# Output sums in the seats of layer A's rows, and one model of the shared port in a planned two-layer attention kernel

## The chip, the core and the metric

The kernel runs on one core of a Trainium2 chip. A core has TensorE (PE in the profile, its weight loads PEld), VectorE (DVE), ScalarE (ACT), GpSimd (POOL) and SyncE (SP), each with a queue of its own that it works through in order, and 16 DMA engines. The metric is the device time of one execution in microseconds (us); the result compared is the median of several runs.

## The reference, cut to what matters

Two attention layers over 2048 rows of 1024 numbers, 32 heads of 32 each, with a projection to q, k, v before and one by `wo` behind. Layer A sees eight rows, two apart; layer B a window of 256 rows. All is in 32-bit floats, and the results stand side by side.

```python
    def _A_ref(x, wqkv, wo):
        H = 32; W, dil = 8, 2
        qkv = ...x @ wqkv...
        idx = pos[:, None] - (jnp.arange(W) * dil)[None, :]
        logits = jnp.einsum("bhsd,bhswd->bhsw", q, kg) * scale
        attn = _softmax(jnp.where(idx >= 0, logits, -1e9), axis=-1)
        o = jnp.einsum("bhsw,bhswd->bhsd", attn, vg)
        return o... @ wo
    def _B_ref(x, wqkv, wo):
        scores = jnp.einsum("bhqd,bhkd->bhqk", q, k) * (Dh ** -0.5)
        mask = (idx[:, None] - idx[None, :] >= 0) & (idx[:, None] - idx[None, :] < 256)
        p = _softmax(jnp.where(mask, scores, -1e9), axis=-1)
        return jnp.einsum("bhqk,bhkd->bhqd", p, v)... @ wo
    return jnp.concatenate([a, b], axis=-1)
```

## The kernel before

**Tiles and stages.** The work is cut into eight units of 512 rows: four of layer B (the dense units), then four of layer A, whose rows are reordered so that its window is eight neighbouring rows. Each unit has eight head groups of four heads. A weight or an input arrives as 32-bit floats in a `raw` tile and is split into a rounded part (a cast, L276 on ScalarE or L279 on VectorE) and the rest (a subtraction, L282 on VectorE); a product is then three matmuls on PE. PE's accumulators are three PSUM banks of ring `g` for projections, four of ring `s` for scores and one bank `o` for attention times values.

**Dense units.** For each head group the scores go to a bank `s`; VectorE takes the row maximum (L1395), ScalarE the exponential (L1400), and the bank is free. Then the logarithm of the sums (L1413 to L1421) is put into the keys and queries, the scores are computed a second time, ScalarE writes the exponentials to `pbuf` (L1480), and the edges of the window are set to zero in `pbuf`: each such mask runs on GpSimd (L1459, affine_select) or on VectorE (L1462, a minimum with a constant), whichever the planner expects to end first (`keep`). Then PE multiplies by the values into `o`.

**Layer A.** Queries and keys of a head group are written to `nat`, and SyncE copies them into a seat (L608): two seats of 1032 columns, side by side in the memory of `pbuf`, which the dense units no longer need. Scores are 128 small matmuls per head group that read the seat (`s<-pbuf`), softmax is done in the tiles `band`, and the result, spread to `wide`, is multiplied by the values. Two pairs of units then get their output projection by a scheme of seven block products (`product`): their operands are sums of blocks, made by VectorE (L1133) from what was stored to memory (`od`), stored again (`sd`, `td`) and loaded by GpSimd's queue (L221). VectorE adds each product to a running sum (L902). In products 1 and 4 of a pair the sum is an output, and goes to a tile `o` that is stored through ScalarE's queue (L908). Sixteen sums are such. Before the change the tile is, by turns, columns 1024 to 1536 of one of the two `band` tiles when they are no longer in use, or a tile `ost`, of which there is one (`NST` is 1).

**What sets the order.** The program is written out by a planner: `Clock` keeps an expected free time for each engine, and the loop at the end picks the next PE work that is ready by this clock. When an instruction of another engine is issued depends on it, too. `Clock.start` says when an engine may begin. VectorE instructions that share a port with GpSimd (`port=True`) are kept as intervals in `held`, with the latest end in `port["dve"]`. The flag `traced` is set between two marks: from the third head group's projection of the first layer-A unit to the first block product.

Of the kernel before, what the change touches and what calls it, by code (L numbers as in the profile page):

```python
# [7 lines left out]
F32 = mybir.dt.float32  # L8
# [6 lines left out]
P = 128  # L15
NG = 8
NK = 8
S = 512
# [45 lines left out]
class Clock:  # L64
# [21 lines left out]
    def start(self, eng, port, *ready):  # L86

        t = max((self.free[eng],) + ready)
        if eng == "pool" and self.traced:
            t = next((e for s, e in self.held if s <= t + 0.06 < e), t + 0.06)  # L90
        elif eng == "pool":
            t = max(t + 0.06, self.port["dve"])
        elif port:
            t = max(t, self.port["pool"])
        return t
# [196 lines left out]
def kernel(ctx, tc, xs, wqk, wv, wo, outs, units):  # L292
# [3 lines left out]
    U = len(units)  # L296
# [10 lines left out]
    stp = ctx.enter_context(tc.tile_pool(name="stp", bufs=NST))  # L307
# [11 lines left out]
    def mm(out, left, right, **k):  # L319
        issued[0] += 4 if left.dtype == F32 else 2  # L320
        n = int(issued[0] + EXTRA - ASKED) // CHUNK
        if n > asked[0]:
            asked[:] = n, ck.now
        nc.tensor.matmul(out, left, right, **k)  # L324
# [30 lines left out]
    done = {}  # L355
# [102 lines left out]
    where_o = {"ot": 0, "s": 0, "bg": 0}  # L458

    def slot(i):  # L460
        return roomp.tile([P, 1024], F32, tag=f"r{i % NO}", name="r")
# [65 lines left out]
    seats = more[:, :2 * (2 * S + 8)].rearrange("p (b c) -> p b c", b=2)  # L527
    band, wide = [None, None], [None, None]
    halo = [[dram.tile([P, 2, 256], F32, name=f"halo{i}_{s}") for s in range(NG)] for i in range(2)]

    xt, xready, ot, rows, waiting = {}, {}, {}, {}, {}
# [32 lines left out]
    def latest(*ts):  # L564
        return None if any(t is None for t in ts) else max(ts)
# [288 lines left out]
    def product(u, i):  # L854

        out = []
        h = totals.setdefault(u, {})

        def ready(n, k):
            if n == 0 and k == 0:  # L860
                for j in range(2):
                    if ("s", u, i, j) not in held:
                        at = where["p", u, i, "s", j]
                        st.split_to(at + 1)
                        if at not in st.ready:
                            return None
                        held["s", u, i, j] = st.get(at)
            if n % 2 == 0 and k == 0 and ("t", u, i, n // 2) not in held:
                at = where["p", u, i, "t", n // 2]
                st.split_to(at + 1)  # L870
                if at not in st.ready:
                    return None
                held["t", u, i, n // 2] = st.get(at)
            x, r = held["s", u, i, k // 2]
            r = max(r[k % 2], held["t", u, i, n // 2][1])
            return latest(rg.when(), r) if k == 0 else r

        def run(n, k):
            if k == 0:
                h["ps"], h["b"] = rg.take()  # L880
            w, x = held["t", u, i, n // 2][0], held["s", u, i, k // 2][0][k % 2]
            c = S * (n % 2) + P * k
            for t, (a, b) in enumerate(TERMS):
                mm(h["ps"], w[:, a, c:c + P], x[:, b, :], start=(k == 0 and t == 0),
                                 stop=(k == 3 and t == 2))
            if k == 1:
                at = where["p", u, i, "t", 1]
                more_w = [kind for kind, _ in st.items[at + 1:at + 1 + (n + 1 if n else 0)]]
                while more_w.count("w") > 1 + n // 2:
                    more_w.pop()  # L890
                st.split_to(at + 1 + len(more_w))

        def after(n, k):
            if k < 3:
                return
            ps, bank = h["ps"], h["b"]
            if i == 0 and n % 2 == 0:
                h["ac", n // 2] = [slot(8 + 2 * g + n // 2) for g in range(2)]
            a, c = [t[:, S * (n % 2):S * (n % 2) + S] for t in h["ac", n // 2]]

            def add(dst, src):
                nc.vector.tensor_tensor(dst, ps, src, op=ALU.add)  # L902
                return ck.use("dve", 0.61, ck.now + ck.SEM)

            def store(r, col, tile, e):
                def go():
                    if going.pop(key, None):
                        nc.scalar.dma_start(outs[ORDER[u + r], 4 * col + n], tile)  # L908
                        ck.load("store", e)

                key = u, r, col, n
                going[key] = go
                ck.defer(e, go)

            if i in (1, 4):
                for f in list(going.values())[:-1]:
                    f()
                where_o["ot"] += 1
                b = where_o["ot"] % 2
                o = band[b][:, 1024:1536] if where_o["ot"] % 3 and U * NG - 2 + b in done["o"] else stp.tile([P, S], F32, tag="ost", name="ost")  # L920
            if i == 0:
                nc.scalar.copy(a, ps)
                e = ck.use("act", 0.485, ck.now + ck.SEM)
            elif i == 1:
                e = add(o, a)
                store(0, 0, o, e)
            elif i == 2:
                e = add(a, a)
            elif i == 3:
                e = add(c, a)  # L930
            elif i == 4:
                e = add(o, c)
                store(1, 0, o, e)
            elif i == 5:
                e = add(c, c)
                store(1, 1, c, e)
                e = add(a, a)
            else:
                e = add(a, a)
                store(0, 1, a, e)  # L940
            rg.give(bank, e)

        for n in range(4):
            for k in range(4):
                at = (n, k)
                out.append((lambda at=at: ready(*at), lambda at=at: run(*at), 3 * CG, lambda at=at: after(*at)))
        return out
# [611 lines left out]
    for u in range(U):  # L1559
        for s in range(NG):  # L1560
            a, b = attention(u, s)
# [58 lines left out]
    while True:  # L1620
# [3 lines left out]
        for name, seq in seqs.items():  # L1624
# [3 lines left out]
            t = seq[pos[name]].ready()  # L1628
# [8 lines left out]
        if ck.later and (best is None or ck.later[0][0] < best[0]):  # L1637
            t = ck.later[0][0]
# [3 lines left out]
        t, name = best  # L1642
# [54 lines left out]
```

## Time and profile before

| what | us |
|---|---|
| three runs | 1792.06, 1794.24, 1795.07; median 1794.24 |
| the profiled execution | 1793.36 |
| its span, first to last instruction | 1791.7 |
| dense units | about 0 to 1030 |
| layer A and its first products | about 1030 to 1677 |
| products after the last attention | 1677.8 to 1787.5 |

The granted clock over the span is 0.998. The rows of the profile name engine, line and tile; `g`, `s` and `o` are PSUM tiles by ring, `x`, `w` and `r` split operands. A matmul's end is modelled, since matmuls overlap in the array: what PE loses is read from the starts of its matmuls and from its waits. A line of a wait says who waited, for whom, total, count and longest.

### The profile page before, as it was taken

The numbers are of one execution on the slowest core, as the hardware profiler recorded it, in microseconds if no ns is written. First come the engines' busy times: TensorE is split into PE (matmuls) and PEld (weight loads), VectorE is DVE, ScalarE is ACT, GpSimd is POOL, SyncE is SP. The second block draws the span as 40 slices with busy tenths as digits, with TensorE's granted clock in tenths as the row PEclk, the third lists the DMA queues.
The fourth block names the chain that finished last, engine by engine and source line by source line (L and its number), as shares of the span: only waits on it lengthen the run. The fifth ranks groups of instructions, "written<-read, shape, count | busy, mean of one in ns | idle before, by whom it ended". The sixth has DMA issues, their size and how long they took to land.

```text
span 1791.7 us, 38433 instructions
## 1 busy us (share of the span) xinstructions
PE 1771.8 (99%) x14496; PEld 1443.6 (81%) x14496; DVE 1295.5 (72%) x2881; ACT 936.3 (52%) x2332; POOL 412.2 (23%) x962
## 2 busy tenths in 40 slices
PE   9999999999999999999999999999999999999999
PEld 7787777888778888878788788888888887887887
DVE  6777876768867769867678556566577869677966
ACT  5565566555656565656554524533354455455442
POOL 3322323222342223332223410100011101001210
PEclk9999999999999999999999999999999999999999
DMA  8355664644656556555556266666576769848984
GB/s 258 105 149 136 186 168 136 170 136 142 186 141 165 151 134 166 154 146 146 147 136 185 61 189 190 199 201 202 171 232 207 213 181 290 291 139 274 303 318 143
DMA packets 154793, 324.57 MB, mean 181 GB/s; under 512 B 18032, under 2 KB 58992, under 8 KB 154608
## 3 DMA queue, kind: packets, MB, share of 16 engines
q0 software_dynamic: 45792, 166.74, 30.9%
q1 hardware_dynamic: 98736, 137.02, 26.9%
q10 hardware_dynamic: 10080, 18.35, 2.8%
q8 instruction: 115, 1.88, 0.5%
q14 instruction: 70, 0.57, 0.1%
HBM read 201.33 MB, written 53.48 MB: 142 GB/s over the span
## 4 chain that ended last, share of the span: by engine, by line
PE 94%; DMA 2%; DVE 1%; ACT 1%; issue 1%; SPq 0%; DVEq 0%; ACTq 0%; POOLq 0%
PE g L324 74%; PE s L324 13%; PE o L324 7%; DMA outs<-ost 0%; DMA raw<-sd 0%; ACT s L1400 0%; DMA pbuf<-nat 0%; DVE w L282 0%; DMA raw<-wqk 0%; DMA raw<-xs 0%; DMA qst<-nat 0%; ACT w L276 0%; DVE r L1133 0%; DVE qst L1435 0%; DVE x L282 0%
## 5 line engine op out<-in xcount | busy, mean ns | idle before, releaser
L324 PE MATMUL g<-x,w 128*128 128x512 f32 x3552 | 879.1, 394 | 5.3 <-DVE ost L902 3.5
L324 PEld LDWEIGHTS g<-x,w 128*128 128x128 f32 x3552 | 658.6, 189 | 135.2 <-issue 10.7
L282 DVE TENSOR_TENSOR w<-raw,w 128x512 fp32r<-128x512 f32 x510 | 334.4, 697 | 53.7 <-ACT w L276 47.5
L1395 DVE CUSTOM_DVE_ANT_0 s<-s,mask_d 128x384 f32<-128x384 f32 (+2 forms) x512 | 261.8, 554 | 98.4 <-PE s L324 98.0
L1400 ACT ACTIVATE s<-s,nm 128x384 f32<-128x384 f32 (+2 forms) x512 | 274.4, 537 | 109.9 <-DVE nm L1395 103.3
L324 PE MATMUL g<-w,x 128*128 128x256 f32 (+1 forms) x1728 | 306.3, 327 | 0.5 <-DVE w L282 0.5
L1459 POOL TENSOR_SCALAR_AFFINE_SELECT pbuf<-pbuf 128x128 f32<-128x128 f32 (+1 forms) x605 | 219.8, 391 | 315.8 <-ACT pbuf L1480 313.8
L324 PEld LDWEIGHTS g<-w,x 128*128 128x128 f32 x1728 | 255.5, 190 | 25.2 <-DVE w L282 1.7
L324 PE MATMUL g<-r,w 128*128 128x512 f32 x960 | 238.5, 394 | 0.5 <-DVE r L1359 0.5
L1480 ACT ACTIVATE pbuf<-s 128x384 f32<-128x384 f32 (+2 forms) x480 | 203.4, 504 | 64.7 <-PE s L324 62.1
L324 PEld LDWEIGHTS g<-r,w 128*128 128x128 f32 x960 | 177.4, 188 | 36.0 <-DVE r L1359 1.1
L221 POOL DMA_DIRECT2D raw<-wqk x126 | 68.2, 541 | 389.2 <-DVE w L282 275.1
L324 PEld LDWEIGHTS s<-qst,kst 128*128 128x128 f32 x704 | 113.6, 189 | 42.0 <-ACT s L1400 16.8
L324 PE MATMUL s<-kst,qst 96*128 96x384 f32 (+2 forms) x512 | 142.3, 342 | 0.9 <-ACT s L1400 0.7
L324 PE MATMUL s<-qst,kst 128*128 128x256 f32 (+2 forms) x704 | 137.1, 302 | 4.0 <-ACT s L1400 3.2
L279 DVE CAST w<-raw 128x1024 fp32r<-128x1024 f32 x176 | 121.2, 689 | 8.6 <-PE g L324 7.8
L324 PEld LDWEIGHTS s<-kst,qst 96*128 96x128 f32 x512 | 93.6, 189 | 26.1 <-issue 4.5
L276 ACT CAST w<-raw 128x1024 fp32r<-128x1024 f32 (+1 forms) x80 | 82.4, 1037 | 47.9 <-PE g L324 15.9
L1400 ACT ACTIVATION_READ_ACCUMULATOR s<-s,nm 128x1 f32 x512 | 105.4, 206 | 0.0
L1260 ACT COPY wide<-band 32x512 f32<-32x512 f32 x128 | 79.0, 617 | 29.5 <-DVE band L1251 28.0
L324 PE MATMUL o<-pbuf,vbuf 128*32 128x384 f32 (+2 forms) x1408 | 91.1, 389 | 0.0
L625 ACT ACTIVATE nat<-g 128x512 fp32r<-128x512 f32 x64 | 38.3, 598 | 98.1 <-PE g L324 84.9
(91 smaller groups left out, 1428.1 us busy)
## 6 DMA issues: line engine op xcount, KB each, us to landing
raw<-wqk POOLq DMA_DIRECT2D x126, 512.0 KB, 4.7
raw<-wv POOLq DMA_DIRECT2D x60, 512.0 KB, 4.9
qst<-nat SPq DMA_DIRECT2D x96, 256.0 KB, 5.3
kst<-nat SPq DMA_DIRECT2D x96, 256.0 KB, 5.8
raw<-wo POOLq DMA_DIRECT2D x44, 512.0 KB, 4.5
raw<-xs POOLq DMA_DIRECT2D x28, 512.0 KB, 4.5
outs<-ost ACTq DMA_DIRECT2D x39, 256.0 KB, 3.1
kst<-halo SPq DMA_DIRECT2D x72, 128.0 KB, 4.5
```

Source lines behind the costliest of these rows:

```text
L221: (self.nc.scalar if early else self.nc.gpsimd).dma_start(raw if len(ap.shape) == 2 else raw.rearrange("p (a b) -> p a b", a=2), ap)
L276: nc.scalar.copy(t[:, 0, :], raw)
L279: nc.vector.tensor_copy(t[:, 0, :], raw)
L282: nc.vector.tensor_tensor(t[:, 1, c:c + 512], raw[:, c:c + 512], t[:, 0, c:c + 512].bitcast(F32), op=ALU.subtract)
L324: nc.tensor.matmul(out, left, right, **k)
L625: nc.scalar.activation(hl[:, 0, :], ps, AF.Copy, scale=sc)
L1260: nc.scalar.copy(diag[r:r + 32, :, :, c:c + 32], turned[r:r + 32, :, :, 1, :])
L1395: nc.vector.tensor_tensor_reduce(ps[:, :n], ps[:, :n], mask[:, cut:full], scale=-1.0, scalar=BIG, op0=ALU.add, op1=ALU.min, accum_out=nm)
L1400: nc.scalar.activation(ps[:, :n], ps[:, :n], AF.Exp, bias=nm, scale=-1.0, accum_out=sm)
L1459: nc.gpsimd.affine_select(w, w, pattern=[[0, m], [step, n]], compare_op=ALU.is_ge, fill=0.0, base=base, channel_multiplier=chan)
L1480: nc.scalar.activation(w, ps[:, :pack * n].rearrange("p (j n) -> p j n", j=pack), AF.Exp)
```

## The change

Two edits. The first takes away a rule of the planner's clock: GpSimd was expected, outside the two marks, to begin only after the end of the last VectorE instruction on the shared port that the clock knew; now it is expected, everywhere, to begin at once, or at the end of the one such instruction in whose interval it falls. The second gives the sixteen output sums four places of 512 columns in the two seats, in turn (seat 1 first half, seat 0 second half, seat 1 second half, seat 0 first half), once the last scores have been read.

```diff
@@ Clock.start
         t = max((self.free[eng],) + ready)
-        if eng == "pool" and self.traced:
+        if eng == "pool":
             t = next((e for s, e in self.held if s <= t + 0.06 < e), t + 0.06)
-        elif eng == "pool":
-            t = max(t + 0.06, self.port["dve"])
         elif port:
             t = max(t, self.port["pool"])
@@ product, after
                 where_o["ot"] += 1
-                b = where_o["ot"] % 2
-                o = band[b][:, 1024:1536] if where_o["ot"] % 3 and U * NG - 2 + b in done["o"] else stp.tile([P, S], F32, tag="ost", name="ost")
+                if U * NG - 1 in done["scores"]:
+                    b, at = where_o["ot"] % 2, where_o["ot"] // 2 % 2 * S
+                    o = seats[:, b, at:at + S]
+                else:
+                    o = stp.tile([P, S], F32, tag="ost", name="ost")
```

Lines behind the first edit are two lower in the changed kernel and one higher behind the second, so L902 is L900 there, L282 is L280, L324 is L322, and L1395 is L1396.

The order of VectorE around the first four output sums, before (each sum reads a `g` bank and a running sum `r`; L282 splits operands, L1133 makes block sums):

```order
L902 TENSOR_TENSOR ost_18772<-g_18756,r_18587 128x512
L1224 TENSOR_REDUCE nm_18780<-band_11157 128x16
L1226 TENSOR_TENSOR band_11157<-band_11157,nm_18780 128x16x40
L282 TENSOR_TENSOR x_18786<-raw_18648,x_18786 128x512
L282 TENSOR_TENSOR x_18789<-raw_18648,x_18789 128x512
L282 TENSOR_TENSOR x_18792<-raw_18650,x_18792 128x512
L282 TENSOR_TENSOR x_18795<-raw_18650,x_18795 128x512
L902 TENSOR_TENSOR ost_18812<-g_18776,r_18587 128x512
L282 TENSOR_TENSOR w_18822<-raw_18752,w_18822 128x512 x2
L902 TENSOR_TENSOR ost_18833<-g_18815,r_18659 128x512
```

and in the changed kernel:

```order
L900 TENSOR_TENSOR pbuf_110<-g_18756,r_18587 128x512
L1225 TENSOR_REDUCE nm_18779<-band_11060 128x16
L1227 TENSOR_TENSOR band_11060<-band_11060,nm_18779 128x16x40
L280 TENSOR_TENSOR x_18785<-raw_18648,x_18785 128x512
L280 TENSOR_TENSOR x_18788<-raw_18648,x_18788 128x512
L280 TENSOR_TENSOR x_18791<-raw_18650,x_18791 128x512
L280 TENSOR_TENSOR x_18794<-raw_18650,x_18794 128x512
L900 TENSOR_TENSOR pbuf_110<-g_18775,r_18587 128x512
L280 TENSOR_TENSOR w_18820<-raw_18752,w_18820 128x512 x2
L900 TENSOR_TENSOR pbuf_110<-g_18813,r_18659 128x512
```

The instructions stand in the same order; the place that the sums are written to is another, and the three are no longer one tile.

In the dense units the order itself moves. VectorE at the end of a unit, ahead of four score rows (`keep_f`, `keep_d`: masks; `w`: a weight being split; ISA: the row maximum), before:

```order
L629 SCALAR_TENSOR_TENSOR nat_5067<-g_4985,nat_5067 128x512
L1462 TENSOR_TENSOR pbuf_110<-pbuf_110,keep_f_210 128x2x128
L1462 TENSOR_TENSOR pbuf_110<-pbuf_110,keep_d_160 128x128
L1462 TENSOR_TENSOR pbuf_110<-pbuf_110,keep_f_210 128x128
L1462 TENSOR_TENSOR pbuf_110<-pbuf_110,keep_d_160 128x128
L279 CAST w_5139<-raw_4989 128x1024
L282 TENSOR_TENSOR w_5139<-raw_4989,w_5139 128x512 x2
L1395 ISA s_5132,nm_5130<-s_5132,mask_d_173 128x384
```

and in the changed kernel:

```order
L627 SCALAR_TENSOR_TENSOR nat_5102<-g_5049,nat_5102 128x512
L1463 TENSOR_TENSOR pbuf_110<-pbuf_110,keep_f_210 128x2x128
L1463 TENSOR_TENSOR pbuf_110<-pbuf_110,keep_d_160 128x128
L277 CAST w_5169<-raw_5053 128x1024
L280 TENSOR_TENSOR w_5169<-raw_5053,w_5169 128x512 x2
L1396 ISA s_5164,nm_5007<-s_5164,mask_d_173 128x384
```

Two narrow masks have gone from VectorE to GpSimd here. PE at the same place, from the last of the four scores to the matmul that takes the first of their banks again, before:

```order
L324 MATMUL s_5158<-kst1_126,qst1_124 128x384
L324 MATMUL g_5077<-w_5081,x_4755 128x512 x3
L324 MATMUL g_5073<-w_5139,x_4821 128x512 x3
L324 MATMUL g_5077<-w_5139,x_4821 128x512 x3
L324 MATMUL o_5178<-pbuf_110,vbuf2_129 32x128 x4
L324 MATMUL o_5178<-pbuf_110,vbuf2_129 32x256 x4
L324 MATMUL o_5178<-pbuf_110,vbuf2_129 32x384 x4
L324 MATMUL s_5193<-qst0_123,kst0_125 128x384
```

and in the changed kernel:

```order
L322 MATMUL s_5190<-kst1_126,qst1_124 128x384
L322 MATMUL g_5109<-w_5113,x_4850 128x512 x3
L322 MATMUL g_5105<-w_5169,x_4900 128x512 x3
L322 MATMUL o_5203<-pbuf_110,vbuf2_129 32x128 x4
L322 MATMUL o_5203<-pbuf_110,vbuf2_129 32x256 x4
L322 MATMUL o_5203<-pbuf_110,vbuf2_129 32x384 x4
L322 MATMUL s_5218<-qst0_123,kst0_125 128x384
```

One group of three `g` matmuls has moved from here to another place. Over the whole program 33 narrow masks (one block of 128 columns) leave GpSimd for VectorE and 25 wide ones (two blocks) go the other way; the counts of all other work on PE are the same.

## The prediction

> **What bounds the kernel now.** I read the page's busy times first, then the list of waits of PE (TensorE), then the end of the program in the timeline, where the chain of waits leaves PE.
>
> ```profile
> span 1791.7 us, 38433 instructions
> PE 1771.8 (99%) x14496; PEld 1443.6 (81%) x14496; DVE 1295.5 (72%) x2881; ACT 936.3 (52%) x2332; POOL 412.2 (23%) x962
> ```
>
> ```profile
> PE s L324 <- ACT s L1400: 4.5, 7, 1.0
> PE g L324 <- DVE ost L902: 3.5, 1, 3.5
> PE s L324 <- DVE qst L1613: 1.5, 1, 1.5
> PE s L324 <- issue: 1.4, 1, 1.4
> PE g L324 <- DVE x L282: 1.1, 1, 1.1
> PE s L324 <- DVE hl L1421: 0.6, 2, 0.3
> ```
>
> PE is idle for only 1791.7 - 1771.8 = 19.9 us, so a change that leaves its 14496 matmuls alone can win little and must be read from PE's waits. The columns are total, count, longest. One wait of 3.5 us stands out: PE waits for VectorE (DVE), which writes an output sum into the tile `ost`. The timeline shows why.
>
> ```profile
> 1634.26 1.60 PE L324 MATMUL s<-pbuf 32*32 32x40 f32 x128
> ...
> 1640.21 0.69 DVE L902 TENSOR_TENSOR ost<-g,r 128x512 f32<-128x512 f32 x1 [0.95 <-PE g L324]
> ...
> 1642.40 2.49 DVE L282 TENSOR_TENSOR x<-raw,x 128x512 fp32r<-128x512 f32 x4
> ...
> 1647.74 1.04 ACT L276 CAST w<-raw 128x1024 fp32r<-128x1024 f32 x1
> ...
> 1648.82 0.96 PE L324 MATMUL g<-x,w 128*128 128x512 f32 x3
> ...
> 1649.33 1.03 ACT L276 CAST w<-raw 128x1024 fp32r<-128x1024 f32 x1
> 1652.46 0.69 DVE L902 TENSOR_TENSOR ost<-g,r 128x512 f32<-128x512 f32 x1 [7.57 <-DMA outs<-ost]
> 1653.07 1.28 DVE L282 TENSOR_TENSOR w<-raw,w 128x512 fp32r<-128x512 f32 x2
> 1653.30 7.11 PE L324 MATMUL g<-x,w 128*128 128x512 f32 x24 [3.52 <-DVE ost L902]
> ...
> 1657.15 2.86 DVE L1133 TENSOR_TENSOR r<-r 128x512 f32<-128x512 f32 x4
> ...
> 1659.93 0.68 DVE L902 TENSOR_TENSOR band<-g,r 128x512 f32<-128x512 f32 x1
> ...
> 1660.76 15.92 PE L324 MATMUL g<-x,w 128*128 128x512 f32 x69 [0.35 <-DVE band L902]
> ```
>
> The chain of waits has one row for the store between the two sums (start, length):
>
> ```profile
> 1645.62 6.76 DMA outs<-ost
> ```
>
> The first sum is done at 1640.21 + 0.69 = 1640.90. Its store is issued at 1645.62, behind earlier work in ScalarE's queue, and takes 6.76 us. There is one `ost` buffer, so the second sum stands 7.57 us on VectorE; it holds a PSUM bank of ring `g`, and PE, which wants that bank, stands 3.52 us. Then PE is slow as well: 24 matmuls in 7.11 us. The windows give the reason (per stretch: length, busy time of PE, weight loads, VectorE, ScalarE, GpSimd, then granted clock, DMA share, GB/s).
>
> ```profile
> 168.00:172.00 4.00, 3.85 (x16) 2.86 (x17) 3.49 (x9) 3.85 (x12) 2.77 (x5) 1.00 0.24 60
> ...
> 1649.50:1653.20 3.70, 0.28 (x2) 0.00 (x0) 0.73 (x2) 0.86 (x1) 0.00 (x0) 0.95 0.18 70
> 1653.30:1656.30 3.00, 3.00 (x7) 2.45 (x8) 2.01 (x4) 0.58 (x1) 0.53 (x1) 0.51 0.48 178
> 1656.30:1660.00 3.70, 3.70 (x17) 3.00 (x17) 3.60 (x7) 2.19 (x4) 0.53 (x1) 1.00 0.90 244
> 1661.00:1675.00 14.00, 14.00 (x63) 11.55 (x63) 13.21 (x22) 8.56 (x15) 3.17 (x6) 1.00 0.98 342
> ```
>
> For 3 us after the wait PE had 0.51 of its clock. The wait is paid once in idle time and again in slow matmuls. The first row is the stretch behind PE's longest wait for ScalarE, the 1.0 us of the list: there the clock stayed at 1.00.
>
> **The change, part by part.** *Sums in the seats.* It removes the reuse of `ost`. The sixteen sums go round four places of `pbuf`, so each waits for the store of the fourth sum before it. No instruction is added. The orders of PE and VectorE around these rows are the same in both programs but for names, so this term can be read directly.
>
> The pitch of a warm matmul, from the row with 69: 15.92 us, less the last one's drain (its 0.394 us in the page's group less one pitch, 0.17), over 69 is 0.228 us. From 1648.82 to 1660.76 are 27 matmuls in 11.94 us; at 0.228 they take 6.16, so 5.78 us are lost. The three end at 1648.82 + 0.68 = 1649.50, so the first loss lasts to 1653.30: 3.80, of which I leave 0.1 to the switch from the `o` matmuls to the `g` ones. The next 24 would take 5.47 and the next begins 7.46 later: 1.99. The second wait in it is 0.35, and 0.16 more because the view counts from the modelled end of a matmul; so 0.51 is wait and 1.48 the slow clock. Removed: 3.7 + 1.48 = **5.2 us**.
>
> What is late next? I put VectorE's same rows in line without the 7.57. The four x rows end at 1644.89, the second sum at 1645.5 (0.61 from its start to the next row's, 1652.46 to 1653.07). The w rows wait for the ACT (ScalarE) cast that ends at 1647.74 + 1.04 = 1648.78 and end at 1650.06; third sum to 1650.7; second w rows (cast ended 1650.36) to 1651.95; the four L1133 rows, 2.78 from start to next start, to 1654.7; fourth sum to 1655.4. PE, through its 24 matmuls at 1649.50 + 5.47 = 1654.97, wants the bank of that fourth sum: about 0.4 to 0.5 us of wait. So the second wait stays as it is. Bounds of this term: 5.78 saved if it goes too, nothing saved if another stall takes all of it (first rival).
>
> A page of the Trainium skill, TensorE: Matmul & The Clock Gate, section "Part 1: The HAM clock gate", says that the array falls to half rate after about 3.4 us idle and needs about 3.4 us of work to come back. The trace agrees: 3.52 idle, then 0.51. By the page's figure the slow stretch would cost an estimated 3.4 / 2 = 1.7 us and the sum would be 5.4 instead of 5.2.
>
> *The planner's rule for the port.* It changes where the 736 edge masks of the dense units run and, through the planner's clock, the order of nearly everything from early in the first dense unit to the last groups of layer A. The prices:
>
> ```profile
> L1459 POOL TENSOR_SCALAR_AFFINE_SELECT pbuf<-pbuf 128x128 f32<-128x128 f32 x434 | 139.1, 351 | 150.4 <-ACT pbuf L1480 149.5 <-PE g L324 0.4
> L1459 POOL TENSOR_SCALAR_AFFINE_SELECT pbuf<-pbuf 128x256 f32<-128x256 f32 x171 | 82.0, 494 | 165.4 <-ACT pbuf L1480 164.4
> L1462 DVE TENSOR_TENSOR pbuf<-pbuf,keep_d 128x128 f32<-128x128 f32 x42 | 12.6, 300 | 9.5 <-ACT pbuf L1480 8.3 <-POOL pbuf L1459 1.0
> L1462 DVE TENSOR_TENSOR pbuf<-pbuf,keep_d 128x256 f32<-128x256 f32 x28 | 12.0, 449 | 28.7 <-ACT pbuf L1480 28.6
> ```
>
> ```profile
> PEld o L324 <- POOL pbuf L1459: 1.3, 4, 0.4
> ```
>
> GpSimd (POOL) has 605 masks now and 597 after: 434 narrow and 171 wide become 401 and 196, at their shares of busy time (139.1 / 434 = 0.32, 82.0 / 171 = 0.48) 221 us before and 222 after. VectorE's 131 become 139, but 78 narrow and 53 wide become 111 and 28: at 0.30 and 0.45 that is 47 us before, 46 after. So no engine's load changes. GpSimd is 23% busy and its masks cost PE's weight loads 1.3 us in all, so the masks themselves cost nothing on the path; if that cover went, their price is these 1.3 us doubled. What is left is the new order of PE against VectorE and ScalarE. One place by hand, the end of a dense unit, where four score banks are wanted again behind three groups of `g` matmuls and an `o` lot:
>
> ```profile
> 467.45 1.39 DVE L282 TENSOR_TENSOR w<-raw,w 128x512 fp32r<-128x512 f32 x2
> ...
> 468.76 0.55 DVE L1395 CUSTOM_DVE_ANT_0 s<-s,mask_d 128x384 f32<-128x384 f32 x1
> ...
> 471.15 0.56 ACT L1400 ACTIVATE s<-s,nm 128x384 f32<-128x384 f32 x1
> ...
> 471.97 0.96 PE L324 MATMUL s<-qst,kst 128*128 128x384 f32 x4
> ```
>
> The last of the four exponentials ends at 471.71. PE begins at 471.97 and needs that fourth bank three starts later; the x4 row's 0.96 less its last matmul's 0.35 puts it near 472.6: 0.9 us to spare. The change takes one group of three matmuls (0.68 us) out of this cover and two narrow masks off VectorE ahead of the scores (about 0.2 us each as they follow one another). Left: about 0.6. So no wait is made here, none removed. I take **0** for the new order. Its bounds: gain 4.5 + 0.6 (every PE wait for L1400 and L1421 gone), loss the same amount again, so 5 us either way; between these ends I choose the middle because the loads are equal and the margin checked stays positive.
>
> **The sum.** The profiled execution took 1793.36 us, its span and 1.66 around it; it lies 0.88 below the median of the three runs. 1793.36 - 5.2 = 1788.2 on its own time, 1794.24 - 5.2 = **1789.0** on the median.
>
> **The rivals.**
> *The saving is taken back by the next transfers.* The DMA engines are full in the stretch from 1661 (share 0.98). If PE, 5.2 us earlier, met loads that do not come earlier, the time would be 1794.2. Against it: the queues idle at 0.18 in the very gap that goes, and the raw buffers are freed by VectorE rows that move up by more than PE does. That the change does not do what it says (the first four sums waiting for the seats' own loads or score reads) gives the same time; the last score matmuls end some 4 us ahead of the first sum, so little speaks for it (1634.26 + 1.60 against 1640.21).
> *New waits that drop the clock (slower).* At the ends of dense units the cover shrinks as shown, and more masks lie on GpSimd ahead of the last `o` lot. If a wait there grew past the length of the one at 1649.5, each would cost 3.7 + 1.48 = 5.2; the second and third dense unit read alike in the new order, so two at once: 1794.24 - 5.2 + 10.4 = 1799.4. It decides from two such waits on, since one is only the saving given back. For it: PE has 1% of idle time, so nothing absorbs a late bank. Against: the longest dense wait now is 1.0 and kept its clock, and the margin above stays positive.
> *The new order also saves.* The model now lets GpSimd start between VectorE's instructions; if the plan fits the chip better and the waits for L1400 go, 1789.0 - 4.5 = 1784.5.
>
> **How the numbers follow.** Forecast 0.57, saving taken back 0.18, slower 0.12, more saved 0.13. A measurement of this kernel tells 0.2%, 3.6 us, from no change: below 1790.7 is faster, above 1797.8 slower. Of the forecast's 0.57 about 0.06 falls above 1790.7 (a dense loss of 1.7 or more). Faster 0.51 + 0.13 = 0.64, same 0.18 + 0.06 = 0.24, slower 0.12. The range goes from near the rich end, 1784.5, to just past the case of no gain, 1794.5; outside it lie the slower rival and part of the richer one, under 2 in 10. The forecast's own range is 1787 to 1791.
>
> **What would show it.** Right: no PE wait for L900 (the sum's line after) over 1 us, a clock of 1.00 in every window after the last scores, the first four sums about 5 us apart, and a wait of at most 0.6 before the fourth sum's bank. The totals of PE's waits for ScalarE's exponentials stay between 2 and 7 us. Wrong: a wait of PE for raw loads between the fourth sum and the last `o` lot (first rival); a window of clock near 0.5 in the dense units (slower); a span below 1785 with the waits for L1400 gone (richer).

## The result and the profile after

The changed kernel is slower: 1803.15 us (median of 5 runs, 1801.61 to 1804.60) against 1794.24; the ratio is 1.0057, with an interval of 1.0046 to 1.0069. The forecast was 1789.0 with a range up to 1794.5. The profiled execution, the shortest of the five, took 1801.61, its span 1799.9; the page's first lines:

```profile
span 1799.9 us, 38437 instructions
PE 1776.7 (99%) x14496; PEld 1441.5 (80%) x14496; DVE 1301.6 (72%) x2893; ACT 937.1 (52%) x2328; POOL 416.6 (23%) x954
```

The loads of the engines are those of before, as forecast; PE's idle time is 23.2 us, 3.3 more. (Part of what PE lost shows as busy: a slow matmul counts as busy, and so does the modelled end of one that is followed by a short wait.) The end of the program does what the second edit, the seats, was meant to do. The four sums in the timeline of VectorE, then the windows over the same stretch (columns as in the prediction):

```profile
1654.42 0.69 DVE L900 TENSOR_TENSOR pbuf<-g,r 128x512 f32<-128x512 f32 x1 [0.72 <-issue]
...
1659.02 0.68 DVE L900 TENSOR_TENSOR pbuf<-g,r 128x512 f32<-128x512 f32 x1
...
1662.68 0.68 DVE L900 TENSOR_TENSOR pbuf<-g,r 128x512 f32<-128x512 f32 x1
...
1667.27 0.68 DVE L900 TENSOR_TENSOR pbuf<-g,r 128x512 f32<-128x512 f32 x1
```

```profile
1653.00:1657.00 4.00, 4.00 (x19) 3.30 (x18) 3.24 (x5) 1.70 (x4) 0.00 (x0) 1.00 1.02 397
1657.00:1661.00 4.00, 4.00 (x20) 3.30 (x19) 2.71 (x5) 3.88 (x9) 1.06 (x2) 1.00 0.98 356
1661.00:1675.00 14.00, 14.00 (x97) 11.32 (x96) 13.39 (x23) 9.15 (x14) 2.64 (x5) 1.00 1.00 347
```

PE is busy throughout, the clock is 1.00, and no sum waits for a store. What was lost lies elsewhere. PE's list of waits has no long row to point at it:

```profile
PE s L322 <- ACT s L1401: 5.3, 6, 1.2
PE g L322 <- DVE w L280: 1.9, 4, 0.9
PE s L322 <- DVE qst L1614: 1.5, 1, 1.5
PE s L322 <- DVE hl L1422: 1.5, 2, 0.8
```

Its first row was 4.5, 7, 1.0 before. The list of the weight loads' waits tells more, because it also counts waits that a matmul's modelled end covers: before, and then after,

```profile
PEld s L324 <- ACT s L1400: 19.8, 39, 1.2
```

```profile
PEld s L322 <- ACT s L1401: 31.5, 63, 1.7
```

In this list PE meets a score bank that ScalarE has not yet read 63 times, where it was 39. The worst of these meetings is at the end of the second dense unit, in the timeline of PE and then of ScalarE (L1401 is the exponential of a score bank, L623 the copy of a finished projection):

```profile
453.88 1.31 PE L322 MATMUL s<-kst,qst 96*128 96x384 f32 x4
455.03 1.68 PE L322 MATMUL g<-x,w 128*128 128x512 f32 x6
457.96 2.13 PE L322 MATMUL s<-kst,qst 96*128 96x384 f32 x4 [1.25 <-ACT s L1401]
```

```profile
456.75 0.60 ACT L623 ACTIVATE nat<-g 128x512 fp32r<-128x512 f32 x1 [2.05 <-PE g L322]
457.24 0.55 ACT L1401 ACTIVATE s<-s,nm 128x384 f32<-128x384 f32 x1
...
457.80 0.55 ACT L1401 ACTIVATE s<-s,nm 128x384 f32<-128x384 f32 x1
...
458.35 0.56 ACT L1401 ACTIVATE s<-s,nm 128x384 f32<-128x384 f32 x1
...
458.91 0.57 ACT L1401 ACTIVATE s<-s,nm 128x384 f32<-128x384 f32 x1
```

This is a ring. PE fills four banks, and does six matmuls that finish a projection. ScalarE stands idle for 2.05 us, not for the scores but for that projection, since its copy is queued ahead of the four exponentials. When PE ends the projection it wants the four banks at once and has nothing else to do: it waits for the copy and the first exponential (1.25 by the row, 1.42 between starts less the pitch), and then 0.39 for each of the next three, so that four scores take 2.13. VectorE is late there too: its row maxima stand behind the split of the next unit's inputs.

```profile
454.17 0.69 DVE L280 TENSOR_TENSOR x<-raw,x 128x512 fp32r<-128x512 f32 x1
454.77 0.42 DVE L277 CAST x<-raw 128x512 fp32r<-128x512 f32 x1
455.23 0.69 DVE L280 TENSOR_TENSOR x<-raw,x 128x512 fp32r<-128x512 f32 x1
455.84 0.56 DVE L1396 CUSTOM_DVE_ANT_0 s<-s,mask_d 128x384 f32<-128x384 f32 x1
```

ScalarE's copy and exponentials stand at the same distances, to 0.01 us, at the ends of the third and fourth dense unit, with waits of 1.42 at 717.33 and 977.12 (at the fourth the copy is one of layer A, L584). The kernel before has the ring as well, at 450.25 to 451.46, but with one exponential behind the copy; this is the ring's price there, and it is paid once:

```profile
450.25 0.60 ACT L625 ACTIVATE nat<-g 128x512 fp32r<-128x512 f32 x1 [0.66 <-PE g L324]
450.74 0.55 ACT L1400 ACTIVATE s<-s,nm 128x384 f32<-128x384 f32 x1
```

```profile
451.46 0.71 PE L324 MATMUL s<-qst,kst 128*128 128x128 f32 x3 [0.60 <-ACT s L1400]
```

### The profile page after: what moved, and what is told of

The parts are those of the page before. It is cut to its first block, busy times and chain, and to the rows that moved or that the text cites. A ratio compares the mean times of both kernels' runs of the same rounds, so it can differ in the third digit from the quotient of the medians.

```text
span 1799.9 us, 38437 instructions
## 1 busy us (share of the span) xinstructions
PE 1776.7 (99%) x14496; PEld 1441.5 (80%) x14496; DVE 1301.6 (72%) x2893; ACT 937.1 (52%) x2328; POOL 416.6 (23%) x954
## 4 chain that ended last, share of the span: by engine, by line
PE 91%; DVE 3%; DMA 3%; ACT 1%; issue 1%; POOL 1%; SPq 0%; ACTq 0%; DVEq 0%; POOLq 0%
PE g L322 72%; PE s L322 13%; PE o L322 6%; DMA raw<-xs 1%; DVE w L280 1%; ACT s L1401 1%; DMA r<-od 1%; DVE s L1396 1%; DVE qst L1436 1%; POOL pbuf L1460 1%; DVE w L277 1%; DMA pbuf<-nat 0%; DMA raw<-wqk 0%; DVE x L280 0%; ACT pbuf L1481 0%
## 5 line engine op out<-in xcount | busy, mean ns | idle before, releaser
L322 PE MATMUL g<-x,w 128*128 128x512 f32 x3552 | 871.9, 393 | 2.3 <-ACT x L274 0.8
L322 PEld LDWEIGHTS g<-x,w 128*128 128x128 f32 x3552 | 659.2, 188 | 134.0 <-issue 4.4
L280 DVE TENSOR_TENSOR w<-raw,w 128x512 fp32r<-128x512 f32 x510 | 334.7, 698 | 53.9 <-ACT w L274 46.6
L1396 DVE CUSTOM_DVE_ANT_0 s<-s,mask_d 128x384 f32<-128x384 f32 (+2 forms) x512 | 262.0, 555 | 122.0 <-PE s L322 121.1
L1401 ACT ACTIVATE s<-s,nm 128x384 f32<-128x384 f32 (+2 forms) x512 | 273.9, 536 | 118.8 <-DVE nm L1396 114.8
L322 PE MATMUL g<-w,x 128*128 128x256 f32 (+1 forms) x1728 | 312.1, 328 | 1.7 <-DVE w L280 1.6
L1460 POOL TENSOR_SCALAR_AFFINE_SELECT pbuf<-pbuf 128x128 f32<-128x128 f32 (+1 forms) x597 | 224.2, 404 | 259.6 <-ACT pbuf L1481 256.9
L322 PEld LDWEIGHTS g<-w,x 128*128 128x128 f32 x1728 | 257.8, 190 | 28.7 <-DVE w L280 3.5
L322 PE MATMUL g<-r,w 128*128 128x512 f32 x960 | 241.7, 393 | 0.0
L322 PEld LDWEIGHTS g<-r,w 128*128 128x128 f32 x960 | 176.4, 188 | 31.9 <-issue 0.6
L322 PE MATMUL s<-kst,qst 96*128 96x384 f32 (+2 forms) x512 | 148.0, 344 | 7.3 <-ACT s L1401 4.6
L322 PEld LDWEIGHTS s<-qst,kst 128*128 128x128 f32 x704 | 110.0, 189 | 39.7 <-ACT s L1401 16.9
L322 PE MATMUL s<-qst,kst 128*128 128x256 f32 (+2 forms) x704 | 135.9, 305 | 1.4 <-DVE qst L1436 0.8
L322 PEld LDWEIGHTS s<-kst,qst 96*128 96x128 f32 x512 | 93.2, 189 | 35.9 <-ACT s L1401 14.7
L1401 ACT ACTIVATION_READ_ACCUMULATOR s<-s,nm 128x1 f32 x512 | 104.8, 205 | 0.0
L219 POOL DMA_DIRECT2D raw<-wv x60 | 39.5, 659 | 234.7 <-DVE w L280 128.0
L1215 DVE TENSOR_TENSOR band<-s,near 128x160 f32<-128x160 f32 x128 | 32.5, 317 | 84.3 <-PE s L322 84.2
L322 PE MATMUL o<-pbuf,vbuf 128*32 128x384 f32 (+2 forms) x1408 | 91.8, 388 | 0.0
```

The costliest lines, as they stand in the source:

```text
L219: (self.nc.scalar if early else self.nc.gpsimd).dma_start(raw if len(ap.shape) == 2 else raw.rearrange("p (a b) -> p a b", a=2), ap)
L280: nc.vector.tensor_tensor(t[:, 1, c:c + 512], raw[:, c:c + 512], t[:, 0, c:c + 512].bitcast(F32), op=ALU.subtract)
L1215: nc.vector.tensor_tensor(p64()[:, j, :, 24:], banks[j][0][:, :160].rearrange("p (b c) -> p b c", b=4), m, op=ALU.add)
L1396: nc.vector.tensor_tensor_reduce(ps[:, :n], ps[:, :n], mask[:, cut:full], scale=-1.0, scalar=BIG, op0=ALU.add, op1=ALU.min, accum_out=nm)
L1401: nc.scalar.activation(ps[:, :n], ps[:, :n], AF.Exp, bias=nm, scale=-1.0, accum_out=sm)
L1460: nc.gpsimd.affine_select(w, w, pattern=[[0, m], [step, n]], compare_op=ALU.is_ge, fill=0.0, base=base, channel_multiplier=chan)
```

## The experiments

Sixteen kernels were run. The first table has what was measured; each is compared with the kernel before on the same chip, so ratios compare better than medians. "Seats" means the second edit, "rule" the first. The intervals of the last three rows are 0.0010 to 0.0022 either way.

| run | what it is | median us | ratio to before, interval |
|---|---|---|---|
| (the change) | seats and rule | 1803.15 | 1.0057, 1.0046 to 1.0069 |
| e1 | seats alone | 1788.28 | 0.9973, 0.9962 to 0.9983 |
| e2 | rule alone | 1809.53 | 1.0088, 1.0074 to 1.0102 |
| e3 | the change, no GpSimd masks | 1799.66 | 1.0038, 1.0024 to 1.0051 |
| e4 | before, no GpSimd masks | 1791.08 | 0.9991, 0.9982 to 1.0000 |
| e5 | seats, rule in layer A only | 1791.42 | 0.9992, 0.9982 to 1.0003 |
| e6 | seats, rule in the first unit only | 1793.07 | 1.0002, 0.9993 to 1.0012 |
| e7 | the change, no input split for units 2 to 4 | 1798.81 | 1.0035, 1.0022 to 1.0048 |
| e8 | seats, no input split for units 2 to 4 | 1788.31 | 0.9977, 0.9966 to 0.9988 |
| e9 | the change, copy behind at two places | 1802.26 | 1.0054, 1.0037 to 1.0071 |
| e10 | e7 and e9 together | 1793.91 | 1.0009, 1.0000 to 1.0019 |
| e11, e12 | handicap 0.1: seats with new, old rule | 1818.10, 1825.56 | 1.0145, 1.0189 |
| e14, e16 | handicap 0.3: seats with new, old rule | 1805.41, 1787.96 | 1.0074, 0.9977 |
| e13, e15 | handicap 0.4: seats with new, old rule | 1791.87, 1790.53 | 0.9997, 0.9987 |

**Which edit.** e1 is the kernel before with the diff's second edit only, e2 with its first only. The letters of the theories are explained where they first stand in the expectations: from e3 on, P says that PE's new order has too little cover over VectorE and ScalarE, and Q that GpSimd's masks hold up the loads behind them in its queue. The S of e1 and e2 is not the S of e7 and e9.

> The seats for the output sums alone, the planner's clock as before; the order of every engine is that of before, only the place of the sixteen sums differs. Theory G (the seats save what was forecast; the loss comes from the new port model): 5.2 us faster, 1789.0. Rival S (the seats cost something themselves, in stores or in writes to pbuf): 1793 or more. PE's wait for the second sum gone, clock 1.00 behind it.

> The port model alone, the sums in band and ost as before. Theory G: the seats' saving is missing from the changed kernel's time, 1803.2 + 5.2 = 1808.4, with PE's wait for the second ost sum of about 3.5 us in it. Rival S: 1800 or less.

Theory G held in both. The seats save 0.27%, 5 us, and the rule costs 0.88% alone; e2 has PE's wait for the second `ost` sum, 2.9 us. e1 beats both kernels. None of its sums waits for a store, and PE around the first four reads:

```profile
1647.90 6.46 PE L324 MATMUL g<-x,w 128*128 128x512 f32 x27
1654.51 15.88 PE L324 MATMUL g<-x,w 128*128 128x512 f32 x69 [0.16 <-DVE pbuf L902]
```

From start to start these 27 matmuls take 6.61 us, where the kernel before took 11.94: 5.3 us less.

**Are GpSimd's masks what is late?** e3 and e4 take out the mask that GpSimd runs, and keep the planner's account of it, so that every other order stays.

```diff
-                nc.gpsimd.affine_select(w, w, pattern=[[0, m], [step, n]], compare_op=ALU.is_ge, fill=0.0,
-                                        base=base, channel_multiplier=chan)
                 return ck.use("pool", dur_p, r)
```

> The changed kernel with the 597 masks that the planner gives to GpSimd left out, the planner's clock unchanged: the orders of PE, VectorE, ScalarE and SyncE are the changed kernel's, GpSimd's queue holds loads alone. It leaves out those edges of the window in layer B. Theory Q (GpSimd's masks stand ahead of loads in its queue and make them late): the three waits of 1.4 + 0.4 + 0.4 + 0.4 us for score banks at the ends of dense units go or halve, 1794 to 1798. Rival P (PE's new order has too little cover over VectorE and ScalarE, whatever GpSimd does): 1801 to 1803, the waits stay.

> The kernel before with its 605 GpSimd masks left out in the same way, as a control; it leaves out those edges of the window in layer B. Both theories: 1792 to 1794, since PE waits for GpSimd's masks by 1.3 us in all in the profile of before. Under theory Q a saving of over 3 us here would say that the loads stood behind masks in the kernel before as well.

The three waits at the unit ends stay at 1.41 us without a single mask on GpSimd. So the masks, whose place the rule decides, are not what PE waits for there. They are worth 0.2% after and 0.1% before, and both are close to the noise: the interval of e3 overlaps the change's, and that of e4 reaches 1.0000. Two numbers were missed: 1799.66 lies between the ranges of Q and P, and 1791.08 lies 0.9 below the range of e4.

**Where in the program.** In e5 and e6 the rule acts in one part (`turn` is the position of that part's first projection among the products; e6 has `< turn` and the second unit's).

```diff
...
-        if eng == "pool":
+        if eng == "pool" and (self.traced or self.new):
             t = next((e for s, e in self.held if s <= t + 0.06 < e), t + 0.06)
+        elif eng == "pool":
+            t = max(t + 0.06, self.port["dve"])
...
             ck.traced = marks[0] <= pos["g"] < marks[1]
+            ck.new = pos["g"] >= turn
```

> Seats in the changed kernel's way, and the new rule for the port only from the first head group of layer A on; the dense units are planned by the old rule. Theory P (the loss lies at the ends of dense units, where the new order of TensorE has too little cover): nothing is lost here, so the time is that of the seats alone, 1788.3, within 1787 to 1791, and no wait over 0.8 us of TensorE for the exponentials in the dense units. Rival A (the loss is spread over both layers, about in proportion to the time planned by the changed rule): layer A outside the two marks takes a third of the 14.9 us between the two kernels with seats, so 1793 or more.

> Seats, and the new rule only in the first of the four dense units; from the second dense unit on the old rule plans again. Theory P: the ends of the second, third and fourth dense unit have their old cover back, so the waits of 1.4 us there are gone; what is left is the first unit's own loss, about 2 us by the excess of TensorE's starts in the first 300 us, so 1788 to 1792. Rival E (the first unit under the new rule leaves the queues in another phase, and that phase makes the loss in all later units): the waits at the unit ends stay and the time is 1798 to 1804.

By the differences of ratios to e1, layer A has 0.19% (3.4 us) of the rule's 0.84% and the first dense unit 0.29% (5.2); the rest, 0.36% or about 6.5 us, would belong to the second to fourth dense unit. Each figure is uncertain by some 0.15%, 2.7 us. Both single times came out above the ranges of P and below those of A and E, so the three unit ends of P are not the whole loss. The division is not clean either, because a part's order also changes what follows it. In e6, where the rule ends with the first unit, the waits at 712.87 and 968.88 are 0.77 again, as before, but the end of the second unit, some 250 us behind the switch, has two long waits. In e5 PE stands at the start of layer A for a load that the changed kernel does not wait for. So part of the 5.2 and of the 3.4 is not lost in this way in the changed kernel. The rows of PE in e6, then in e5:

```profile
456.19 0.44 PE L325 MATMUL s<-kst,qst 96*128 96x384 f32 x1 [1.25 <-ACT s L1404]
...
459.40 0.45 PE L325 MATMUL s<-kst,qst 96*128 96x384 f32 x1 [0.96 <-ACT s L1404]
```

```profile
983.99 0.76 PE L325 MATMUL s<-kst,qst 96*128 96x384 f32 x3 [2.67 <-DMA kst<-nat]
```

**What makes the unit ends late.** e7 and e8 leave out VectorE's casts and subtractions there; they use the tiles of unit 1 instead.

```diff
-                    t = self.xpool.tile([P, 2, S], F32R, tag="x", name="x") if self.items[i][0] != "xw" else self.sums()
+                    if i in self.cut:
+                        t = self.kept[self.cut[i]][h]
+                    else:
+                        t = self.xpool.tile([P, 2, S], F32R, tag="x", name="x") if self.items[i][0] != "xw" else self.sums()
...
```

> The changed kernel with the split of the inputs of units 2, 3 and 4 left out (they are computed from unit 1's x tiles, so their outputs are not the reference's); all loads and the order of every other instruction are as in the changed kernel. This takes 24 casts and 24 subtractions from VectorE, all at the ends of dense units. Theory P with VectorE as the late engine (the casts and subtractions stand in VectorE's queue ahead of the row maxima there): the three waits of 1.4 us for the exponentials go, with the 0.4 us ones behind them and the clock drops, together 2.6 to 4 us per unit end: 1791 to 1796. Rival S (ScalarE's copy of a projection ahead of the exponentials is what is late): the waits stay above 1 us and the time above 1799.

> Control: the kernel with the seats alone and the old rule, with the same split of the inputs of units 2, 3 and 4 left out (outputs not the reference's). Theory P: the old order has cover enough there, so VectorE's work at the unit ends costs little: 1785.5 to 1788.5, at most 3 us less than with the split. Rival G (VectorE's work at the unit ends costs the same in any order): as large a gain as in the changed kernel, 1776 to 1784.

The waits stayed at 1.42, 1.41 and 1.41, each with its three of 0.39: rival S held for them, and P's number, 1791 to 1796, was missed. S's number, above 1799, was missed too, by 0.2. VectorE's share of these waits is hidden behind the copy. Yet some 4 us went by the ratios (1.0057 to 1.0035, uncertain by 3), and nothing in the control, so the split costs at other places of the new order; one such place comes with e9.

In e9 the copy is held until three of the exponentials behind it are written (its reader on SyncE allows no more), at the second and third unit's end; the fourth is left.

```diff
-            nc.scalar.activation(hl[:, 0, :], ps, AF.Copy, scale=sc)
+            def copy():
+                nc.scalar.activation(hl[:, 0, :], ps, AF.Copy, scale=sc)
+
+            if (u, s, t) in BEHIND:
+                behind.append([4, copy])
+            else:
+                copy()
...
```

> The changed kernel with one ScalarE instruction moved at two places: at the ends of the second and third dense unit (the waits at 457.96 and 717.33) ScalarE's copy of a finished projection, L623, goes behind the next three exponentials instead of ahead of them; the third such place, at 977.12, is left as it is. Every other order is unchanged. Theory S (the copy waits for TensorE's last group of the projection, the exponentials wait behind the copy, and TensorE waits for the exponentials with nothing left to do between): the two waits of 1.42 us fall to what VectorE's late row maxima still cost. The first maximum ends at 456.4, an exponential takes 0.56, so TensorE could go on at about 457.1: 0.5 to 0.7 us of wait; the one at 977 stays 1.4. Time 1 to 4 us below the changed kernel, 1799 to 1802.5. Rival P (VectorE's order alone): the waits stay at 1.4.

> The edit of the run before and, with it, the split of the inputs of units 2, 3 and 4 left out (outputs not the reference's), so that neither the copy nor VectorE's casts and subtractions stand ahead of the four exponentials. Theory S and P together (two causes in line, each hidden by the other): the first two waits go altogether, 0.3 us or less each, with the three of 0.4 us behind them and the clock drop at 718; the one at 977 stays 1.4. Time 3 to 6 us below the run without the split alone (1798.8): 1793 to 1796. If a third thing holds the exponentials, the waits stay above 0.8.

e9's timeline of PE at the second unit's end:

```profile
455.86 1.56 PE L323 MATMUL s<-kst,qst 96*128 96x384 f32 x3 [0.50 <-ACT s L1418]
...
458.03 0.44 PE L323 MATMUL s<-kst,qst 96*128 96x384 f32 x1 [0.61 <-ACT s L1418]
```

The wait fell to the 0.5 that VectorE's late maxima leave, as S says, and one of 0.6 remains before the fourth bank, whose exponential is behind the moved copy. The time, 1802.26, lies in the range expected, but at 0.5 us below the change, uncertain by some 3.7, it does not tell S from no gain. In the profiled execution the clock fell behind the shortened wait all the same (0.50 in the window 459.2 to 462.6), and a wait of 2.25 us came up ahead of the third unit's end, where the changed kernel's profile has none. VectorE's timeline there:

```profile
704.12 0.43 DVE L278 CAST x<-raw 128x512 fp32r<-128x512 f32 x1 [3.20 <-DMA raw<-xs]
...
706.26 0.56 DVE L1413 CUSTOM_DVE_ANT_0 s<-s,mask_d 128x384 f32<-128x384 f32 x1
```

VectorE stands for an input load, and the row maxima that PE needs stand behind the split. The moved copy did not make this wait: e2 and e14, with the same PE rows at this place, show it too, 1.77 us at 707.91 and 1.76 at 709.44. In the profiles of e7 and e10, without the split, it is not there. So the new order is open to a late input load at this place, which may be part of what e7 won; no run tests that alone. With both causes out (e10) the second unit's end reads:

```profile
452.98 0.88 PE L330 MATMUL s<-kst,qst 96*128 96x384 f32 x4
453.70 1.55 PE L330 MATMUL g<-x,w 128*128 128x512 f32 x6
455.09 1.21 PE L330 MATMUL s<-kst,qst 96*128 96x384 f32 x3
456.91 0.45 PE L330 MATMUL s<-kst,qst 96*128 96x384 f32 x1 [0.61 <-ACT s L1425]
```

The first score follows the projection without a wait and the next two nearly so (three take 1.21); the fourth still meets the copy, which I had forgotten in the expectation (0.3 or less). The place left alone keeps its 1.41 at 971.67. The ratio fell from e7's 1.0035 to 1.0009, 4.7 us for one instruction moved at two places, and by 8.6 us from the changed kernel's (each uncertain by about 3). So two causes stood in line at these waits, ScalarE's copy and VectorE's split, and with either one left the waits did not go.

**The rule or the order?** The planner has a constant, `MASK_BIAS`, a handicap in us for a mask on GpSimd. Other values give other orders under either rule (all with the seats).

```diff
-MASK_BIAS = 0.2
+MASK_BIAS = 0.1
```

> The changed kernel with one constant of the planner at another value: the handicap that a mask gets on GpSimd (0.2 us) is 0.1. The rule for the port is the new one; the order of all engines changes somewhat in the dense units. Theory R (the new rule itself gives worse orders, since GpSimd's masks do in fact wait for VectorE): the time stays near the changed kernel's, 1799 to 1806. Theory L (the rule only reshuffles, and the changed kernel drew a bad order at the unit ends, which repeats in three units): the time moves by several us, to 1790 to 1798, and the waits of 1.4 us at the unit ends are gone.

> The kernel with the seats alone and the old rule, with the same constant at 0.1: an order as different from that kernel's as the new rule's is. Theory R: the old rule gives good orders, 1786.5 to 1790. Theory L: the order found with 0.2 under the old rule is a lucky one of many (the kernel's constants were chosen with it), and another order costs 2 to 8 us: 1790 to 1796.

Neither theory's numbers came. The constant moved some 170 to 220 masks to VectorE (GpSimd kept 429 and 385, where the change has 597 and the kernel before 605), so the loads changed and these two say nothing clean on the order alone, except that the old rule is not the better one as such: here it is 0.43% slower than the new. At 0.3 and 0.4 the loads stay close (e13: 653 masks on GpSimd).

> The changed kernel with the planner's handicap for a mask on GpSimd at 0.4 instead of 0.2. The rule is the new one; GpSimd gets 656 masks instead of 597. At the ends of the dense units the order is another: behind the projection that ScalarE must copy, TensorE has one score and then twelve or more products, where the changed kernel has four scores at once. Theory O (the loss is in the order at a few places, most of all these unit ends, and not in the rule): no wait over 1 us at 458, 717 and 977, and 1787 to 1793. Theory R (the rule gives worse orders everywhere): 1797 to 1806.

> The changed kernel with the same constant at 0.3. The order differs from the changed kernel's in some 90 places of TensorE, but the four scores behind the copied projection stand at all three unit ends as there. Theory O: the waits of 1.4 us are there, and 1799 to 1806. If the time is below 1796 with these waits in place, they are not what costs the most.

> Control: seats alone, old rule, the constant at 0.4 (630 masks on GpSimd by the count of the program's rows, 610 with 0.2). Unit ends ordered as in the kernel before (one score of 384 columns and then small ones behind the copied projection, a wait of 0.77). Theory O: 1786 to 1791. If it is 1793 or more, any change of the order costs, whatever its unit ends.

> Control: seats alone, old rule, the constant at 0.3; the order differs from that of the seats alone in 24 places of TensorE. Theory O: 1786 to 1790, with the 0.77 waits at the unit ends. 1793 or more would say that small reshuffles alone cost as much.

All four fell into the ranges of theory O. Under the new rule with 0.4 the unit's end has one score behind the finished projection, then products; PE's timeline:

```profile
453.24 0.86 PE L322 MATMUL g<-x,w 128*128 128x512 f32 x3
454.36 0.44 PE L322 MATMUL s<-kst,qst 96*128 96x384 f32 x1 [0.26 <-ACT s L1401]
455.26 3.07 PE L322 MATMUL g<-x,w 128*128 128x512 f32 x11 [0.47 <-DVE w L277]
```

With 0.3 the four scores are back, with the waits (PE's timeline, then windows behind it):

```profile
455.70 1.69 PE L322 MATMUL g<-x,w 128*128 128x512 f32 x6
458.63 2.19 PE L322 MATMUL s<-kst,qst 96*128 96x384 f32 x4 [1.25 <-ACT s L1401]
460.62 3.56 PE L322 MATMUL g<-x,w 128*128 128x512 f32 x8
```

```profile
458.60:461.00 2.40, 2.01 (x5) 1.19 (x6) 2.37 (x6) 1.77 (x7) 0.14 (x1) 0.91 0.59 198
461.00:464.00 3.00, 3.00 (x8) 2.31 (x7) 2.93 (x13) 2.00 (x7) 0.58 (x1) 0.50 0.54 149
464.00:468.00 4.00, 4.00 (x20) 3.33 (x19) 3.94 (x9) 0.47 (x2) 0.72 (x1) 1.00 0.23 45
```

Here the clock fell as well, and eight matmuls of 0.228 took 3.0 us: another 1.2 lost in this window, and about 1.7 in the whole slow stretch (cut to 460.6 to 464.0, the window reads 0.50). The price of the rule, as new ratio over old, is 0.9957 at 0.1, 1.0084 at 0.2, 1.0097 at 0.3 and 1.0010 at 0.4 (uncertain by about 0.003 at 0.1 and 0.0015 to 0.002 at the others). It has no sign of its own. It is dear in the two of the three pairs with nearly unchanged loads in which the new order has the four scores at the unit ends. That fits theory O and does not prove it, since these orders differ at many other places too. (At 0.1 the new order has them too, with waits of 1.42 at 457.92 and 717.62 against L's expectation, but there both orders lose more elsewhere.)

## Why the prediction was wrong

**The seats' term was right.** 5.2 us were forecast, and 1794.24 x (1 - 0.9973) = 4.8 measured, with 3.0 to 6.8 by the interval; the signs named for it are there (no wait for L900 over 1 us, a clock of 1.00 behind the last scores, sums 3.7 to 4.6 us apart in the change and 4.6 to 5.0 in e1). The second wait, which was to stay at 0.4 to 0.5 us, stayed in e1: its 27 matmuls take 6.61 us instead of 6.16. In the change it is gone.

**The step that failed** is the last of the planner's term: "So no wait is made here, none removed. I take 0 for the new order." Its bound of 5 us was too small as well: the order costs 0.84%, 15 us. Three things were wrong in it.

First, one place was worked out by hand and stood for all. Even there the margin was thinner than the 0.6 worked out: in the profile after the fourth exponential ends at 477.61 and PE's fourth score starts at 477.78, 0.17 later, so no wait of PE stands there, but only just. The costly place lies nearly 20 us ahead (457.96 against 477.12 for the first of these scores). It was in view: the 0.60 at 451.46 is one of the seven waits in the list's first row. Had that wait been followed back through ScalarE's queue, to the copy at 450.25 that waited for PE, the question would have been how many exponentials stand behind that copy in the new order: one before, four after. The order of the program answers this without a run.

Second, the reason "the loads are equal" bears on busy time alone. The busy times did stay equal, VectorE's to 0.5% and GpSimd's to about 1%; the loss is in who stands ahead of whom.

Third, the bounds were taken from PE's own waits (4.5 + 0.6). They miss the short waits that the weight loads' list shows, and the clock, which fell behind waits below the 1.0 us that had kept it in the kernel before (last section).

**The rivals.** The slower one, with a chance of 0.12, was nearest: new waits at the ends of dense units, alike from unit to unit. Its mechanism was half right. The waits are 1.42 and three of 0.39 each, not the 3.5 it asked for, and the masks that it put ahead of the `o` lot had no part in them (e3). Its sign, a clock near 0.5 in the dense units, came: 0.50 from 202.4 to 205.8. Its price of 10.4 us was still too low against 15. "Saving taken back" is refuted by e1 and by the windows above, where DMA is full and PE busy. "The new order also saves" is refuted by the price of the order. The sign that the waits for exponentials stay "between 2 and 7 us" was useless: they came to 5.3, and the time was lost all the same.

**What stays open.** Of the 15 us, two unit ends and the input split account for 8.6, uncertain by 3 (e10 against the change). In the two profiled executions, compared matmul by matmul, e10 ends 6.9 us ahead, and 3.5 of it arise at the two unit ends; the rest is spread, and part of it is the clock. The first unit's 5.2 and layer A's 3.4 are differences of times that do not add up cleanly, and were not followed to single instructions; for the first unit PE's timeline suggests the same kind of thing, waits of 0.95, 1.10 and 0.87 between 178 and 202 and a low clock behind them, but no run took them away.

## What to carry to other kernels

When a planner's rule changes and the loads stay equal, look for rings in the new order: an engine's instruction that waits for PE, queued ahead of work that PE needs next. Count what stands behind it: once PE has nothing else to do, it goes on at the pace of that engine (here 0.56 us a score, where PE alone takes 0.17). A constant tuned with one rule is tuned to the order it drew: compare rules over several values of it (here the price ran from -0.4% to +1.0%), and try each of two edits alone, since here one gained 5 us and the other hid it.

## What the runs showed of the hardware

The granted clock fell behind waits much shorter than the 3.5 us of the kernel before. In the changed kernel, after waits of 0.45, 0.39, 0.87 and 0.39 between 199 and 202 (taken between the starts of matmuls, less their pitch), the windows read:

```profile
199.00:203.00 4.00, 2.93 (x9) 1.94 (x10) 3.97 (x10) 3.40 (x13) 0.72 (x1) 0.92 1.08 229
203.00:206.40 3.40, 3.40 (x10) 2.66 (x10) 3.29 (x10) 1.63 (x7) 0.21 (x1) 0.59 1.10 293
206.40:210.00 3.60, 3.60 (x20) 2.97 (x19) 1.62 (x9) 1.03 (x4) 0.52 (x1) 1.00 0.72 230
```

PE was idle for a quarter of 4 us, in pieces below 1 us, and then had 0.59 of its clock for 3.4 us. It does not follow each time: behind the 1.25 us at 457.96 the changed kernel kept 1.00 in its profiled execution, where e14 with the same waits fell to 0.50.

```profile
457.90:461.00 3.10, 2.69 (x9) 1.74 (x10) 3.07 (x9) 1.80 (x8) 0.72 (x1) 1.00 0.50 159
461.00:464.00 3.00, 3.00 (x16) 2.43 (x15) 2.90 (x12) 2.47 (x8) 0.00 (x0) 1.00 0.57 175
```

Over the profiles of the change, e2, e3, e7, e11 and e14 at the three unit ends, and of e9 and e10 at the one left alone, the clock fell behind 14 of 20 such waits, but in the changed kernel's profile behind none of its three. So that profile, 1.5 us below the kernel's median, may well show too little of this cost.

The Trainium skill's page TensorE: Matmul & The Clock Gate, section "Part 1: The HAM clock gate", puts the fall after one idle window of about 3.4 us. These rows differ: no idle stretch of that length precedes the falls, and the measurement decides. The length of the slow stretch agrees with the page: the windows cut to 202.4 to 205.8 in the changed kernel and to 460.6 to 464.0 in e14 read 0.50 over 3.4 us.
